# A long convolution beside a gated MLP on one core: the loads of the later chunks issued by GpSimd into its own queue

## The chip, the core and the metric

The kernel runs on one core of a Trainium2 chip. A core has five engines that work through instruction streams of their own, each in order: TensorE (PE in the profile, its weight loads PEld), VectorE (DVE), ScalarE (ACT), GpSimd (POOL) and SyncE (SP). They wait for each other through semaphores. Transfers between the main memory and the core's own memory run on 16 DMA engines. An instruction of SP, ACT or POOL starts them, and the profile shows those of SP as SPq. The metric is the time on the device in microseconds (us); less is better.

## The reference, cut to what matters

```python
xn = layernorm(A_q)                              # 2048 rows of 640, bf16
# part A: a long convolution with gates
k_shift = sum over t<4 of k[s-t] * shift_k[:, t] # a short filter along the rows
kv = k_shift * v
y  = irfft(rfft(kv padded) * rfft(ssm_k padded)) # each column with its filter of 2048 taps
y  = y + kv * ssm_D
A  = xn * y
# part B: a gated MLP, 640 -> 1728 -> 640
B  = (sigmoid(xn @ w_gate) * (xn @ w_up)) @ w_down
out = A_q + A + B
```

## The kernel before, in words

**Rows and blocks.** A row index is written p·16 + b, with p one of 128 partitions and b one of 16 blocks. x, xn, k, v and the result have this form in the core's memory. Four blocks make a group, and the MLP runs over the four groups t = 0 to 3.

**The MLP.** For each group TensorE needs xn transposed (`xnT`). Group 0 is transposed on TensorE; for groups 1 to 3 a DMA transpose of each block does it (`xn_turn`, L240, issued by SP). For each of 13 slices of the hidden width, `gate_mm` and `up_mm` (five matmuls each, `product`, L260) fill one bank each of a pool of four in the matmul memory (`psG`); ACT takes the sigmoid (`gate_ev`, L269), DVE multiplies (`up_ev`, L275) into `hT`. A shared last slice is `both_*`. `down_mm` (L304) multiplies hT by `wd`, seven matmuls a call, and `down_ev` (L309, DVE) adds the result to x in place.

**The layer norm.** Per group: statistics (`ln_norms`, DVE L198 and L202), variance (`ln_var`, L210), the power −1/2 on POOL (`ln_pow`, L214), and `ln_xn` (DVE, L219) for each block.

**The convolution.** The columns are five chunks of 128. For each chunk c:
- loads: the filter `hn` in four DMAs and the D row `dr` (`load_h`, L136 and L139), the four taps of the short filter for all partitions (`load_taps`, L143), k in two halves (`load_k`, L155) with three rows from the partition before in two DMAs (`load_halo`, L159 and L160), and v in two halves (`load_v`, L169). k has two buffers (`kxs`, used by turns), v with the filter has two (`kvh`), and `hn`, `dr` and the taps have one each;
- `taps` (ACT, for chunk 0 POOL), sixteen steps `kv_op` on DVE (L337 to L346; eight for each half of the blocks), two transposes of the filter on DVE (`h_turn`, L323), and `add_D` on POOL (L317), which adds D to the filter's first tap;
- a transform in two stages by matmuls: `st1_mm` (eight calls, TensorE L363 and L365; those for block 0 wait for `add_D`), evacuated by `st1_ev`, written to main memory (`wr1`, L377) and read back in another layout (`rd2`, L387), `st2_mm` (L396) and `st2_ev`;
- the product of the two spectra on DVE (`prod`, L409 and L411), `inv1_mm` (L425), `inv1_ev`, again a trip through main memory (`wr2`, L441 and L445; `rdb`, L455), `inv2_mm` (L464, with the table `TBt`), and two DVE steps (`inv2_q` L469, `inv2_x` L474) that multiply with xn and add to x.

**The order.** Nothing is scheduled automatically. Each kind of step has a letter and a list of its own (`chains`), and the string `ORDER` says, letter by letter, which list gives the next step. The letters' order is therefore the program order, and with it the order on each engine and on each queue. `g` stands for gate, up and down products, `s` and `u` for their evacuations, `m` for the first loads, `n` for x's groups 2 and 3 and the table `TBt`, `h`, `T`, `K`, `V` for the chunk loads from chunk 2 on (taps from chunk 1), `k` for `kv_op`, `P` and `D` for the two POOL steps, `e` for the transposes, `w`, `r`, `W`, `R` for the trips through main memory. `F`, `J` and `I` are evacuations of `st2`, `inv1` and `st1` done by DVE instead of ACT. A step waits only for the data and buffers that it uses, but on its engine it stands behind every earlier step.

In the kernel before, SP issues all these transfers: 137 steps of these lists. POOL's list is nine steps long: taps 0, add_D 0, pow 1, add_D 1, add_D 2, pow 2, add_D 3, add_D 4, pow 3. (`pow 1` is `ln_pow` of group 1, and so on.)

Of the kernel before, what the change touches and what calls it, by code (L numbers as in the profile page):

```python
# [19 lines left out]
P = 128  # L20
NB = S // P
# [36 lines left out]
def kernel(  # L58
# [14 lines left out]
    nc = tc.nc  # L73
    xr = A_q.flatten_outer_dims().rearrange("(p b) d -> p b d", b=NB)
    kr = A_k.flatten_outer_dims().rearrange("(p b) d -> p b d", b=NB)
    vr = A_v.flatten_outer_dims().rearrange("(p b) d -> p b d", b=NB)
# [3 lines left out]
    Drow = A_ssm_D.rearrange("(o d) -> o d", o=1)  # L80

    s1bits, tbbits, smbits = _tables()
    srow = A_shift_k.rearrange("d m -> (d m)").rearrange("(o n) -> o n", o=1)
    S1d = nc.inline_tensor(s1bits, name="tabS1")
    TBd = nc.inline_tensor(tbbits, name="tabTB")
# [4 lines left out]
    dr = ctx.enter_context(tc.tile_pool(name="dr", bufs=1, space=bass.MemoryType.DRAM))  # L90
# [8 lines left out]
    TBt = res.tile([P, 2, NB, P], U16, name="TBt")  # L99
# [12 lines left out]
    kxs = [res.tile([P, NB + 3, P], BF16, name="kx%d" % i) for i in range(2)]  # L112
# [8 lines left out]
    sync = nc.sync  # L121
# [3 lines left out]
    cin = [dict() for _ in range(NC)]  # L125

    def load_x(eng, g, n=4):
        for b in range(4 * g, 4 * g + 4, n):
            eng.dma_start(x[:, b:b + n, :], xr[:, b:b + n, :])

    def load_h(c):

        d = cin[c]
        d["hn"] = cv.tile([P, 4, 512], BF16, name="hn")
        d["dr"] = cv.tile([1, P], BF16, name="dr")
        sync.dma_start(d["dr"][:, :], Drow[:, c * P:(c + 1) * P])  # L136
        for q in range(4):
            src = A_ssm_k[c * P:(c + 1) * P, 512 * q:512 * q + 512].rearrange("(k r) t -> r k t", k=4)
            sync.dma_start(d["hn"][32 * q:32 * q + 32, :, :], src)  # L139

    def load_taps(c):
        cin[c]["sraw"] = cv.tile([P, 4 * P], BF16, name="sraw")
        sync.dma_start(cin[c]["sraw"][:], srow[:, 4 * c * P:4 * (c + 1) * P].to_broadcast((P, 4 * P)))  # L143

    def taps(c):
        sc = cv.tile([P, 4, P], BF16, name="sc")
# [5 lines left out]
        cin[c]["sc"] = sc  # L152

    def load_k(c, lo, hi):
        sync.dma_start(kxs[c % 2][:, lo + 3:hi + 3, :], kr[:, lo:hi, c * P:(c + 1) * P])  # L155

    def load_halo(c):
        cs = slice(c * P, (c + 1) * P)
        sync.dma_start(kxs[c % 2][16:P, 0:3, :], kr[15:P - 1, NB - 3:NB, cs])  # L159
        sync.dma_start(kxs[c % 2][1:16, 0:3, :], kr[0:15, NB - 3:NB, cs])  # L160

    def slot(c):

        if "kvh" not in cin[c]:
            cin[c]["kvh"] = cv.tile([P, 2, NB, P], BF16, name="kvh", bufs=2)
        return cin[c]["kvh"]

    def load_v(c, lo, hi):
        sync.dma_start(slot(c)[:, 0, lo:hi, :], vr[:, lo:hi, c * P:(c + 1) * P])  # L169

    def load_w(eng, lo, hi, u):
        if u == 0:
# [348 lines left out]
    def step(k, fn, *args):  # L521
        chains[k].append((fn, args))
# [16 lines left out]
    def hs(c):  # L539
        return [(load_h, c)]  # L540

    def ks(c):
        return [(load_halo, c), (load_k, c, 0, 8), (load_k, c, 8, NB)]

    def vs(c):
        return [(load_v, c, 0, 8), (load_v, c, 8, NB)]

    for k in ((load_w, sync, 512, 768, 0),
              (load_w, sync, 512, 768, 1),
              (load_taps, 0),  # L550
              (sync.dma_start, SMt[:], SMd.ap()),
              (load_w, sync, 768, 1024, 0),
              (load_w, sync, 768, 1024, 1),
              (load_w, sync, 1024, 1280, 0),
              (load_w, sync, 1024, 1280, 1),
              (load_wd, sync, 0, 7),
              *ks(0),
              (load_w, sync, 1280, FF, 0),
              (load_w, sync, 1280, FF, 1),
              *hs(0),  # L560
              *vs(0),
              (load_wd, sync, 7, NFC),
              (sync.dma_start, S1t[:], S1d.ap()),
              *hs(1),
              (load_x, sync, 1),
              *ks(1),
              *vs(1)):
        step("m", *k)
    for k in ((load_x, sync, 2), (load_x, sync, 3), (sync.dma_start, TBt[:], TBd.ap())):
        step("n", *k)  # L570
    step("Z", taps, 0)

    for c in range(NC):
# [28 lines left out]
        if c == 0:  # L602
            continue
        step("T", load_taps, c)
        step("t", taps, c)
        if c > 1:
# [21 lines left out]
    step("o", store, NB - 1, NB, 4 * P, DM)  # L628

    ORDER = """  # L630
    mgmmmmgmgmgsummZmgmgsmmgugmssgkmmukgskgugkusgsugkkgkHggmmuskuggkHmssukgmDgggukskgukkksaTmmgauAgmkaAH
    HlglAalAlglmwgautAkagugmggPmwlkgAhglkelauleggkakukkugekAAuuDkHgkuaaekgkwgsATKugkAwgsnkkgskgtuKaKAuka
    gskkgauwgkAlDAakVgglkKkrsakAuwAgakgVsAgalswAkaguKgkkAurbgkBswksHgTBgkbtuguBBpkgawkgslaAgsuKkalupKgrA
    AgkahPlnHsAwugaglVasgkgVpAsTAKukDpuckwglkkCgaCaHAugkAkgkeklubkgrkBBgguuwkgbggkpghtBBrbkegleBgBaauegw
    HAparguVkApauAkgwpADWaugakksAngkugpkwlAsucgsgJlpkCulbrgBKBsgaAuapgpAgrbsFggBussWkukrlpcHgguPCCgbslkV
    ggBuBgbpslBkuBRdpgspgWqqcusdgCgkrkkrCsbqFugqBgubskgBRdwBuagpAaqAdgllWwrsewRpugaqgIaggrpAaAaqupgIqupg
    ddcCgeuqgJebgupegFRuBgqbBpgqBgWpdcrguqqgJqCrubwuwdrgFpBgsbqpggpWpqBugBpscsuJggCurpgbggRFBbsWpdsudupq
    rgBqgqBcqRJsgrpCgsbBuWguBpdspqgbuBBgpqdpsgcgrugCRJqbpggsduBqsBgupgspgWqRqcuJdqgsgCdoqgusqWgudggqgugo
    uRgquRggddouqqgguqddgqqqqoquqggoogouoogouoooo
    """  # L640
    left = {k: iter(v) for k, v in chains.items()}
    for k in "".join(ORDER.split()):
# [33 lines left out]
```

## Time and profile before

| | us |
|---|---|
| median of 3 runs (238.31 to 239.72) | 238.9 |
| the profiled execution | 237.94 |
| its span, first to last instruction | 236.2 |
| PE busy | 229.1 (97%) |
| DVE busy | 204.1 (86%) |
| ACT busy | 121.7 (52%) |
| POOL busy | 11.5 (5%) |
| mean busy share of the DMA engines, SP's queue | 90.3% |

The granted TensorE clock is 1.0 throughout. A busy time counts what an engine executes; DMA issues are not counted. In a line of the timeline the numbers are the start, the duration, the engine, the line of the program, the operation with what it writes and reads, a count, and in square brackets the idle time before it with what ended it. In the waits a line gives who waited for whom: the total, the number of times, the longest.

### The profile page before, as it was taken

Reading aid. Unit: us, or ns where it says so; the run is one execution under the profiler, and the core shown is the slowest. Engines: PE = TensorE matmul, PEld = TensorE weight load, DVE = VectorE, ACT = ScalarE, POOL = GpSimd, SP = SyncE. Lnnn points to the kernel's source line nnn. Section 1 sums busy time; section 2 is a strip of 40 time slices with the busy share of each in tenths; the row PEclk is TensorE's granted clock in tenths of the full one; section 3 lists DMA queues with packets and bytes.
Section 4 is the critical chain, followed back from the end, with each engine's and each line's share of the span. In section 5 each row is a group of like instructions: output and inputs, shape, how many; then the busy total and the mean of one; then the engine's idle time right before and its main releaser. Section 6 shows DMA issues by size and latency. Waiting matters only on the chain.

```text
span 236.2 us, 5433 instructions
## 1 busy us (share of the span) xinstructions
PE 229.1 (97%) x2205; PEld 131.2 (56%) x2205; DVE 204.1 (86%) x364; ACT 121.7 (52%) x152; POOL 11.5 (5%) x24
## 2 busy tenths in 40 slices
PE   7799999999899899999999999999999999999995
PEld 3664445877355445666754444478664344446772
DVE  3632898999969999999999999899999999988473
ACT  2343323633564897776776777653346367653000
POOL 5210000020100001000100010000000000000000
PEclk9999999999999999999999999999999999999999
DMA  6999999958899999899899996899989879556664
GB/s 211 292 313 237 259 308 299 257 174 163 223 317 269 321 253 270 225 286 217 228 232 321 248 265 186 240 246 271 235 260 284 238 186 255 160 155 177 191 212 134
DMA packets 97183, 56.79 MB, mean 240 GB/s; under 512 B 55878, under 2 KB 91270, under 8 KB 96902
## 3 DMA queue, kind: packets, MB, share of 16 engines
q1 hardware_dynamic: 96214, 55.62, 90.3%
q10 hardware_dynamic: 944, 0.82, 1.1%
q8 instruction: 17, 0.28, 0.5%
q14 instruction: 8, 0.07, 0.1%
HBM read 36.12 MB, written 18.35 MB: 231 GB/s over the span
## 4 chain that ended last, share of the span: by engine, by line
PE 84%; DVE 8%; DMA 4%; issue 1%; ACT 0%; ACTq 0%; DVEq 0%
PE pg L260 23%; PE pu L260 23%; PE pd L304 20%; PE psb L464 4%; PE ps L396 3%; DMA w<-in_B_w_up_dram 3%; PE ps L363 3%; PE ps L365 3%; PE psa L425 2%; PE pg L281 1%; DVE st L198 1%; DVE tmp L341 1%; DMA xnT<-xn 1%; DVE acc L343 1%; PE pu L251 1%
## 5 line engine op out<-in xcount | busy, mean ns | idle before, releaser
L260 PEld LDWEIGHTS <-w 128*128 128x128 bf16 x500 | 46.5, 98 | 55.8 <-issue 6.8
L304 PE MATMUL pd<-wd,hT 128*128 128x320 bf16 (+2 forms) x448 | 65.3, 299 | 0.0
L260 PE MATMUL pg<-xnT,w 128*128 128x512 bf16 x250 | 62.2, 380 | 0.9 <-DMA xnT<-xn 0.9
L260 PE MATMUL pu<-xnT,w 128*128 128x512 bf16 x250 | 62.2, 380 | 0.8 <-DVE hT L275 0.8
L304 PEld LDWEIGHTS <-hT 128*128 128x128 bf16 x448 | 41.9, 98 | 18.2 <-issue 2.3
L223 ACT CAST t<-ps 128x1024 bf16<-128x1024 f32 x38 | 37.8, 1016 | 23.6 <-PE ps L365 16.0
L269 ACT ACTIVATE sig<-pg 128x512 bf16<-128x512 f32 x52 | 31.1, 603 | 30.7 <-PE pg L260 27.7
L223 ACT CAST xz<-ps 128x1024 bf16<-128x1024 f32 x35 | 34.2, 1015 | 20.3 <-PE ps L396 20.3
L275 DVE TENSOR_TENSOR hT<-sig,pu 128x512 bf16<-128x512 bf16 x52 | 34.8, 675 | 9.6 <-PE pu L260 5.6
L411 DVE TENSOR_TENSOR xz<-xz 128x2048 bf16<-128x2048 bf16 x20 | 24.3, 1215 | 0.1
L365 PE MATMUL ps<-kvh,S1t 128*128 128x128 bf16 x160 | 21.7, 220 | 0.0
L363 PE MATMUL ps<-kvh,S1t 128*128 128x128 bf16 x160 | 21.6, 218 | 0.0
L341 DVE TENSOR_TENSOR tmp<-kx,sc 128x1024 bf16<-128x1024 bf16 x30 | 20.5, 683 | 0.4
L343 DVE TENSOR_TENSOR acc<-acc,tmp 128x1024 bf16<-128x1024 bf16 x30 | 20.5, 684 | 0.4
L309 DVE TENSOR_TENSOR x<-pd,x 128x320 bf16<-128x320 f32 (+2 forms) x32 | 15.2, 483 | 5.9 <-PE pd L304 5.7
L363 PEld LDWEIGHTS <-S1t 128*128 128x128 bf16 x160 | 15.5, 97 | 2.8 <-DVE kvh L346 0.3
L365 PEld LDWEIGHTS <-S1t 128*128 128x128 bf16 x160 | 15.4, 96 | 2.6
L198 DVE BATCH_NORM_STATS2 st<-x 128x6 f32<-128x320 bf16 x32 | 13.9, 476 | 2.7 <-DMA x<-in_A_q_dram 2.7
L469 DVE TENSOR_TENSOR yx<-psb,xn 128x512 bf16<-128x512 f32 x20 | 13.7, 684 | 1.4 <-PE psb L464 1.0
L409 DVE STREAM_SHUFFLE xz<-xz 128x512 f32<-128x512 f32 x20 | 14.5, 725 | 0.0
L223 ACT CAST ao<-psa 128x1024 bf16<-128x1024 f32 x11 | 10.8, 1014 | 5.8 <-PE psa L425 5.6
L464 PEld LDWEIGHTS <-TBt 128*128 128x128 bf16 x160 | 9.8, 98 | 3.0 <-issue 1.5
(48 smaller groups left out, 149.3 us busy)
## 6 DMA issues: line engine op xcount, KB each, us to landing
d<-t SPq DMA_DIRECT2D x20, 512.0 KB, 5.3
t<-d SPq DMA_DIRECT2D x20, 512.0 KB, 5.7
bi<-d SPq DMA_DIRECT2D x8, 512.0 KB, 4.8
d<-ao SPq DMA_DIRECT2D x6, 512.0 KB, 5.6
kx<-in_A_k_dram SPq DMA_DIRECT2D x10, 256.0 KB, 5.3
hn<-in_A_ssm_k_dram SPq DMA_DIRECT2D x20, 128.0 KB, 5.2
kvh<-in_A_v_dram SPq DMA_DIRECT2D x10, 256.0 KB, 5.4
x<-in_A_q_dram SPq DMA_DIRECT2D x3, 640.0 KB, 6.4
```

The costliest lines, as they stand in the source:

```text
L198: nc.vector.bn_stats(d["st"][:, i, s2, :], x[:, b, s2 * 320:(s2 + 1) * 320])
L223: nc.scalar.copy(out=out, in_=in_)
L260: nc.tensor.matmul(pg[:, :], lhsT=w[:, c, u * UP + fc * P:u * UP + (fc + 1) * P], rhs=xnT[:, :, c, :], start=(c == 0), stop=(c == NC - 1))
L269: nc.scalar.activation(sig[fc][:, :], pgs[0, fc][:, :], ACT.Sigmoid)
L275: nc.vector.tensor_tensor(hT[:, fc, :], sig[fc][:, :], pgs[1, fc][:, :], ALU.mult)
L304: nc.tensor.matmul(pd[:, :], lhsT=hT[:, fc, bb * P:(bb + 1) * P], rhs=wd[:, fc, es], start=(fc == 0), stop=(fc == NFC - 1))
L341: nc.vector.tensor_tensor(d["tmp"][:, :, :], kx[:, lo + 3 - m:hi + 3 - m, :], sb(m), ALU.mult)
L343: nc.vector.tensor_tensor(d["acc"][:, :, :], d["acc"][:, :, :], d["tmp"][:, :, :], ALU.add)
L363: nc.tensor.matmul(ps[:, i, 0:P], lhsT=S1[:, b, h, :], rhs=cin[c]["kvh"][:, 0, b, :], start=True, stop=True)
L365: nc.tensor.matmul(ps[:, i, P:2 * P], lhsT=S1[:, b, h, :], rhs=hp[:, b // 2, b % 2, :], start=True, stop=True)
L411: nc.vector.tensor_tensor(z[:, 1:3, :, :], z[:, 0:1, :, :].to_broadcast((P, 2, 8, P)), z[:, 1:3, :, :], ALU.mult)
L464: nc.tensor.matmul(ps[:, i, :], lhsT=TB[:, h, 4 * m + i, :], rhs=bi[:, h, 4 * (m % 2) + i, :], start=(h == 0), stop=(h == 1))
```

## The change

A helper `queue(c)` gives GpSimd's queue for chunks 2 to 4 and SP's for chunks 0 and 1, and every chunk load is issued through it. x's groups 2 and 3 and the table `TBt` are issued by GpSimd as well. That makes 39 DMA issues: for each of three chunks five of `load_h`, one of `load_taps`, two of `load_halo`, two each of `load_k` and `load_v`; two for x; one for the table.

```diff
+    def queue(c):
+        return nc.gpsimd if c > 1 else sync
+
     def load_h(c):
 ...
-        sync.dma_start(d["dr"][:, :], Drow[:, c * P:(c + 1) * P])
+        queue(c).dma_start(d["dr"][:, :], Drow[:, c * P:(c + 1) * P])
         for q in range(4):
 ...
-            sync.dma_start(d["hn"][32 * q:32 * q + 32, :, :], src)
+            queue(c).dma_start(d["hn"][32 * q:32 * q + 32, :, :], src)
 
     def load_taps(c):
 ...
-        sync.dma_start(cin[c]["sraw"][:], srow[:, 4 * c * P:4 * (c + 1) * P].to_broadcast((P, 4 * P)))
+        queue(c).dma_start(cin[c]["sraw"][:], srow[:, 4 * c * P:4 * (c + 1) * P].to_broadcast((P, 4 * P)))
 ...
     def load_k(c, lo, hi):
-        sync.dma_start(kxs[c % 2][:, lo + 3:hi + 3, :], kr[:, lo:hi, c * P:(c + 1) * P])
+        queue(c).dma_start(kxs[c % 2][:, lo + 3:hi + 3, :], kr[:, lo:hi, c * P:(c + 1) * P])
 
     def load_halo(c):
         cs = slice(c * P, (c + 1) * P)
-        sync.dma_start(kxs[c % 2][16:P, 0:3, :], kr[15:P - 1, NB - 3:NB, cs])
-        sync.dma_start(kxs[c % 2][1:16, 0:3, :], kr[0:15, NB - 3:NB, cs])
+        queue(c).dma_start(kxs[c % 2][16:P, 0:3, :], kr[15:P - 1, NB - 3:NB, cs])
+        queue(c).dma_start(kxs[c % 2][1:16, 0:3, :], kr[0:15, NB - 3:NB, cs])
 ...
     def load_v(c, lo, hi):
-        sync.dma_start(slot(c)[:, 0, lo:hi, :], vr[:, lo:hi, c * P:(c + 1) * P])
+        queue(c).dma_start(slot(c)[:, 0, lo:hi, :], vr[:, lo:hi, c * P:(c + 1) * P])
 ...
-    for k in ((load_x, sync, 2), (load_x, sync, 3), (sync.dma_start, TBt[:], TBd.ap())):
+    for k in ((load_x, nc.gpsimd, 2), (load_x, nc.gpsimd, 3), (nc.gpsimd.dma_start, TBt[:], TBd.ap())):
         step("n", *k)
```

The string `ORDER` is another one, too, with the same 845 steps. What follows from it on each engine:

- POOL's list has 33 steps: taps 0, halo 2, add_D 0, first half of k 2, add_D 1, pow 1, h 2, taps 2, x 2, first half of v 2, second half of k 2, second half of v 2, taps 3, halo 3, add_D 2, k 3 (first half), x 3, h 3, TBt, k 3 (second half), pow 2, v 3 (first half), halo 4, v 3 (second half), add_D 3, taps 4, k 4 (first half), h 4, v 4 (first half), add_D 4, k 4 (second half), pow 3, v 4 (second half).
- SP keeps the first loads, the chunks 0 and 1, the transposes, the trips through main memory and the stores, 113 steps. The transposes of group 1 stand behind the first half of v 1; the second half follows after them. `add_D 1` now precedes `pow 1` on POOL.
- PE has the same steps in another order in places: the first `st1_mm` of chunk 0 comes after three down calls of group 0 instead of one, the first `inv1_mm` after four down calls of group 1 instead of two, `st1_mm` of chunk 3 after six down calls of that group instead of four; some calls of stage 2 and of the second inverse stage are one to five places earlier or later.
- DVE and ACT follow these moves. DVE takes 15 evacuations instead of 14 (one of stage 1 fewer, one of stage 2 and one of the first inverse stage more), ACT one fewer. The second transpose of chunk 2's filter stands before the statistics of x's blocks 9 to 11 instead of behind two of them.

More of the change, by code (lines that the diff above doesn't have):

```diff
@@ L630 @@
     ORDER = """
[L631 to L639, printed above, removed]
+    mmmmmmmmmggggsmmsumggsguuZsgggmukksmgmskmukgkggkmuksHgsggumkuggskgukHgskgmkmuggmkTsksgKuugkDagaAgkmA
+    uaHKtHmwmagllllAglgDPkAuaAwmklllahuelgekAugekakkugaggAgkggkAakaukuewgkukmkkgsTggAkuwsngkVutAgaskwkgs
+    AKgaukgrHkaAgAualakswkgAagVguskrAgAbgkwTksuBkBskkguKDgskkHlkaagguAlAKkngbtwushungpkplBsBgaAwgaugkpKl
+    gksaupgAAPlglswkVslrgkuKaueaglHAwaggkkAAVDcwCggTkaCkukuaAgregHkkAbggkugBBKkuurpbBgeklgBkgpbpgBluBpeg
+    atawAkuWggskuaklpghuAwasgAAgaarluAkHrkggAcVskgkJupgsCbgDswBugkBuspaAaKklgPgpAbugBkFsWrgRkcVCCsgugpdH
+    rsbpBkgBugWqudbsgplkpgrBBcurgqRCsqJgbgWkwgukgswpBrBlubksBFqgusludapdqaglgeAaguggRqAeaquAwAappgAaepqe
+    ggIcgCuwguJbBgpFdgrbpqugWBuqdpqBrgcugJpqgrCbugpsRwBFggpbupgBdsrqBuWpgdqrcJspggqgCbuFRqBggsubpdsWugBB
+    gdprscCqgpJrqgbsuBgqFRgupsgbspudpgqrWBgBduqqRcpgJCqWgsqbsBugBgpugsRdpgpucsgqJqCWdgqgusqgudgqouggudRq
+    gqugoRogggqudguodqgqqdudoggqqqqgogqoouuoooooo
     """
```

## The prediction

> **What bounds the kernel now.** I read the page's busy times and slices first, then the windows by stage, the waits, and the timelines of SyncE's queue (SP), VectorE (DVE) and GpSimd (POOL).
>
> ```profile
> PE 229.1 (97%) x2205; PEld 131.2 (56%) x2205; DVE 204.1 (86%) x364; ACT 121.7 (52%) x152; POOL 11.5 (5%) x24
> ...
> DVE  3632898999969999999999999899999999988473
> ...
> DMA  6999999958899999899899996899989879556664
> ```
>
> ```profile
> core 0: us, PE busy (x) PEld busy (x) DVE busy (x) ACT busy (x) POOL busy (x), PEclk, DMA share, GB/s
> ...
> 37.00:60.00 23.00, 22.12 (x203) 16.48 (x202) 22.56 (x46) 9.74 (x11) 1.41 (x2) 1.00 0.89 208
> 60.00:80.00 20.00, 19.18 (x135) 10.58 (x135) 17.46 (x33) 12.19 (x17) 0.72 (x1) 1.00 0.99 285
> 80.00:100.00 20.00, 20.00 (x191) 10.54 (x189) 19.74 (x35) 15.70 (x20) 1.43 (x2) 1.00 0.94 255
> ...
> 200.00:220.00 20.00, 20.00 (x220) 10.71 (x205) 16.92 (x27) 9.34 (x12) 0.00 (x0) 1.00 0.56 157
> ```
>
> TensorE (PE) is full; DVE is nearly full from 30 to 200 us; the DMA engines are busy about nine tenths. POOL is idle. PE's own work is not touched by the change, so a gain can only come out of PE's waits, and they are few:
>
> ```profile
> DVE acc L337 <- DMA kx<-in_A_k_dram: 4.7, 2, 2.9
> ...
> PE pg L260 <- DMA xnT<-xn: 0.9, 1, 0.9
> ...
> PE pu L260 <- DVE hT L275: 0.8, 1, 0.8
> ```
>
> After 20 us these two PE waits are the only ones over 0.3 us. The first, at 59.1 us, opens block 1: its last transpose is late. SP's timeline says why:
>
> ```profile
> 50.55 0.26 SPq L136 DMA_DIRECT2D dr<-in_A_ssm_D_dram  x1
> 50.90 2.35 SPq L139 DMA_DIRECT2D hn<-in_A_ssm_k_dram  x4
> 53.36 5.27 SPq L240 DMA_TRANSPOSE xnT<-xn  x4
> ...
> 62.16 2.63 SPq L155 DMA_DIRECT2D kx<-in_A_k_dram  x2
> ```
>
> The first normalised block was ready at 50.84 (DVE L219), but chunk 2's filter load stood ahead of the transposes; its D row waited for POOL's add of chunk 1, which itself ran behind `pow`. The second PE wait, at 76.8 us, is DVE being late, and DVE had lost time here:
>
> ```profile
> 69.21 0.69 DVE L337 TENSOR_TENSOR acc<-kx,sc 128x1024 bf16<-128x1024 bf16 x1 [1.73 <-DMA kx<-in_A_k_dram]
> ```
>
> Chunk 2's k was issued at 62.16 and DVE stood 1.73 us for it.
>
> **The change, part by part.** The sum is against the profiled execution, 237.94 us with a span of 236.2; the median of the runs is 238.9, 0.96 above it, and I add that at the end.
>
> *Off SP.* 39 DMA issues leave SP (per chunk 5 of h, 1 of taps, 2 of halo, 2 of k, 2 of v, three times; x twice; TBt). SP's rows for them add up to some 30 us between 50.5 and 134. Block 1's transposes then follow from xn's first tile: 51.0 + 5.27 for four + 1.4 from the last issue's end (58.63) to PE's start (60.05) = 57.7, and PE had finished its earlier work at 59.1. The wait of 0.9 goes whole; what is late next is PE itself. Of the other moves past SP (wr1's writes and rd2's reads run sooner by an issue or two) PE has no wait to recover: 0.
>
> *Chunk 2's k early.* On POOL it needs only k buffer 0, free after DVE's last read of it at 40.6. That halos wait for the rows they overwrite alone is seen in SP's row of 82.57 (chunk 4's halo), before the last DVE read of the same buffer at 83.03. So k of chunk 2 lands long before 67.5, DVE gets 1.73 us back, and PE's 0.8 goes: −0.8.
>
> *What an issue costs POOL.* No row shows one. Ends: SP's fastest issue of the same k load, 0.39 us, and SP's slowest, 2.93. For a value I take POOL's only element-by-element row: `pow` takes 0.563 us on one column and 1.016 on four, so 0.412 + 0.151 a column of 128. A load of 1,024 runs of 256 B (half of a k or v chunk) is 8 columns for the source and 8 for the target: 0.41 + 16 x 0.151 = 2.83. One of 128 runs (a quarter of h, taps, x, TBt): 0.71. Both halo loads: 1.7. One h group with its D row: 3.3. The value sits at the upper end, since the software row is nearer in kind. All 39: 3 x (4 x 2.83 + 3.3 + 0.7 + 1.7) + 2.1 = 53 us, inside 110 us in which POOL computes 5: POOL has room, and only its order can hurt. Queued behind a POOL load are `add_D` (TensorE's stage 1 waits for it), `pow` (the xn tiles on DVE wait for it) and the next loads. Place by place, with the times of before:
>
> - add_D 0 behind chunk 2's halo: released near 29.6, done by 32; stage 1 of chunk 0 starts after 40. Nothing.
> - pow 1 behind k of chunk 2 and add_D 1: 40.6 + 2.83, add_D 1 at 44.2; pow's input comes at 49.0. Nothing.
> - pow 2 behind h 3 (which needs DVE's second transpose of chunk 2's filter), TBt and k: 3.3 + 0.7 + 2.8 = 6.8. In the new order DVE has between that transpose and the first xn of group 2, start to start in its timeline, 3 statistics of 1.0, 5 convolution steps and 5 hT products of 0.60, and two shuffles and products of 0.62 + 1.14: 12.6 us. With pow's own 1.0 that leaves 4.8.
> - add_D 3 behind va3, halo 4, vb3: from pow 2's end at 91.95, 2.83 + 1.7 + 2.83 + 0.42 = 99.7. Stage 1 of chunk 3, now two down products later, starts near 102.4. 2.7 to spare; this place decides from 2.83 + 1.35 = 4.2 us a k or v load.
> - second half of k, chunk 4, behind add_D 4: 0.42 + 2.83 + the landing. SP's k loads landed 3.7 to 4.9 us (shortest, median) after issue, with 0.5 of it the issue: 6.5 to 7.7. Between the filter transpose that frees add_D 4 and the step that needs this half DVE has 4 x 0.60 + 3 x 0.60 + 1.14 + 0.62 + a cast of 1.14 = 7.1. A wait of 0 to 0.6, taken as 0.3.
>
> *xn beside POOL's issues.* POOL now writes while DVE normalises. That the two engines exclude each other is in POOL's rows:
>
> ```profile
> 49.11 1.02 POOL L214 TENSOR_TENSOR rstd<-var,mhalf 128x4 f32<-128x4 f32 x1 [17.25 <-DVE var L210]
> 50.10 0.42 POOL L317 TENSOR_TENSOR kvh<-kvh,dr 1x128 bf16<-1x128 bf16 x1
> 60.10 0.72 POOL L317 TENSOR_TENSOR kvh<-kvh,dr 1x128 bf16<-1x128 bf16 x1 [9.58 <-DMA xnT<-xn]
> ...
> 114.36 1.16 POOL L317 TENSOR_TENSOR kvh<-kvh,dr 1x128 bf16<-1x128 bf16 x1 [19.22 <-DMA xnT<-xn]
> ```
>
> The add of 0.42 took 0.72 and 1.16 where DVE ran a two-input operation, and ended 0.28 us after that one's end both times (60.54 and 115.24). The other way round, DVE's operations beside pow at 49.11 kept their length (0.68 and 0.49). So the price on DVE lies between 0 and every xn of groups 1 and 2 waiting for a load being written: 3 x 0.71 behind h 2, then 1.6 left of va3 and 2.83 of vb3, 6.5 together. I take one such meeting, 0.7: pow 1 releases the first xn and POOL's next load at the same moment. The Trainium skill, "SBUF — State Buffer", section "Who interferes with whom", goes further: a VectorE operation in a two-port mode, which tensor_scalar can enter, and a GpSimd operation lock each other out for the whole instruction. By that rule the term is nearer 6.5 than 0.7; the rows beside pow don't bear it out for DVE's side.
>
> *Two queues, one set of DMA engines.* The bytes are the same. Loads start earlier and share with the round trips (d<-t 5.3 us to landing, t<-d 5.7). PE waits for none of them now, so there is nothing to gain; taken as 0, the other end being the 3 us of the rival below.
>
> *The steps moved.* PE's list is the same set in another order. One evacuation goes from ACT to DVE: +1.22 there, inside the 3 us that DVE has free between 120 and 200. If that cover is gone, +1.2.
>
> Sum: −0.9 − 0.8 + 0.3 + 0.7 = −0.7, so 237.2 for a profiled execution and 238.2 beside the median.
>
> **Rivals.**
>
> *POOL falls behind (slower).* If a k or v load costs POOL over 4.2 us, add_D 3 holds PE. At 5 us and 0.71: +1.6 there (two loads of 0.8 more), +2.2 at k of chunk 4, less what overlaps, some +3; at 6 us and 1.2 a plain load, pow 2's group takes 6.0 + 1.2 + 6 = 13.2 and the 12.6 us are used up, va3 and k of chunk 3 are late too: +10 and over. Times 241 to 250. For it: software writes the runs, and no row bounds it. Against: POOL's columns cost 0.15.
>
> *xn held out (slower).* The 6.5 of above in stretches where DVE is busy 22.56 of 23 and 19.74 of 20, so most of it passes on: 238.2 − 0.7 + 2 to 6.5, about 241.5.
>
> *Transfers collide (slower).* Early loads take a turn each on engines that are 0.9 busy. If each round trip lands 1 us later, the last groups of a chunk come late where stage 2 has least room, 2 to 3 us in all: 240.5 to 241. The Trainium skill, "DMA: Bandwidth & Descriptors", section "Issuing engines are not separate DMA queues", speaks this way: issuing from several engines saves only issue time. That the trace agrees is seen in the one place where issue time did cost something, the transposes.
>
> *It does not do what it says.* DVE or PE take the freed time in other small waits, as both are full anyway: 238.9.
>
> *Whole gain.* Both waits go, no meeting costs anything: 238.9 − 1.7 = 237.2. Below 236.9 there is nothing to take.
>
> **How the numbers follow.** Within 0.5% is 1.2 us either way, about what a measurement of this kernel can tell from no change. The forecast, with its small prices anywhere between nothing (the whole gain) and twice the value, has 0.48 and a range of its own of 237.0 to 239.3; half of it lies below 237.7: 0.24 faster, 0.24 same. No effect 0.12, same. POOL behind 0.21, of it 0.01 too little to be told (same); xn held out 0.11 and collision 0.08. Slower 0.20 + 0.11 + 0.08 = 0.39, same 0.24 + 0.12 + 0.01 = 0.37. The likeliest single case is the forecast, 238.2. The range goes from the floor, 236.9, to 243.5, which leaves out the larger prices of the first rival.
>
> **What the changed profile would show.** Right: no PE wait for xnT near 59; no DVE wait for kx near 67 to 69; POOL issue rows of 0.4 to 2.9 us; add_D 3 done before stage 1 of chunk 3. Wrong: a PE wait of L363 on POOL L317, a DVE wait of L219 on POOL L214, L219 longer than 0.45 us, L337 waiting for kx after 120, or landings of t<-d well over 5.7.

## The result, and the profile after

The changed kernel took 252.75 us (median of 6 runs, 251.01 to 255.5) against 238.97 us for the kernel before (6 runs): a ratio of 1.0552, 95% interval 1.0513 to 1.0591. The ratios here and below leave out single slow runs (here the one of 255.5 us), while the times are medians of all runs. The forecast was 238.2 us with a range to 243.5: the time is 14.6 us above it and outside the range. Lines of the changed program carry numbers 3 higher than before from `load_h` on (L263 is the product that was L260).

The page of the changed kernel, busy times, slices and DMA queues (packets, MB, time of the packets as a share of 16 engines' span):

```profile
span 250.1 us, 5454 instructions
...
PE 231.9 (93%) x2205; PEld 132.4 (53%) x2205; DVE 206.2 (82%) x365; ACT 120.4 (48%) x151; POOL 39.9 (16%) x63
...
PE   8799999994089999999979999999999999999994
...
PEclk9999999999569999999999999999999999999999
...
q1 hardware_dynamic: 79900, 47.86, 73.6%
q0 software_dynamic: 2448, 7.77, 12.7%
```

PE has two slices of standstill after 58 us, and a lower granted clock behind them. The windows name the stage (the rows answer those shown of before):

```profile
core 0: us, PE busy (x) PEld busy (x) DVE busy (x) ACT busy (x) POOL busy (x), PEclk, DMA share, GB/s
37.00:60.00 23.00, 22.11 (x204) 16.44 (x201) 22.53 (x45) 9.53 (x11) 9.43 (x13) 1.00 0.93 227
60.00:80.00 20.00, 10.56 (x46) 4.65 (x47) 8.27 (x14) 4.57 (x7) 1.87 (x3) 0.74 0.77 162
80.00:100.00 20.00, 19.90 (x161) 10.36 (x160) 18.67 (x35) 15.33 (x21) 6.39 (x10) 1.00 0.81 247
```

From 60 to 80 us PE worked 10.56 us where it had worked 19.18. The waits of PE, and its timeline where it starts again:

```profile
PE pg L263 <- DMA xnT<-xn: 11.3, 2, 10.3
...
PE ps L399 <- DMA t<-d: 1.1, 1, 1.1
```

```profile
69.44 2.29 PE L263 MATMUL pg<-xnT,w 128*128 128x512 bf16 x5 [10.33 <-DMA xnT<-xn]
71.53 2.16 PE L263 MATMUL pu<-xnT,w 128*128 128x512 bf16 x5
```

Block 1's products, at 60.05 us before, start at 69.44, after a wait of 10.33 us for the transposes, and their first two groups of five take 2.29 and 2.16 us where 1.24 is usual. The two queues' timelines around it, SP's and POOL's:

```profile
51.16 6.79 SPq L243 DMA_TRANSPOSE xnT<-xn  x4
```

```profile
50.58 0.61 POOL L139 DMA_DIRECT2D dr<-in_A_ssm_D_dram  x1
51.20 2.36 POOL L142 DMA_DIRECT2D hn<-in_A_ssm_k_dram  x4
53.55 0.56 POOL L146 DMA_DIRECT2D sraw<-in_A_shift_k_dram  x1
54.10 0.57 POOL L129 DMA_DIRECT2D x<-in_A_q_dram  x1
54.64 0.93 POOL L172 DMA_DIRECT2D kvh<-in_A_v_dram  x1
55.54 0.91 POOL L158 DMA_DIRECT2D kx<-in_A_k_dram  x1
56.42 0.91 POOL L172 DMA_DIRECT2D kvh<-in_A_v_dram  x1
```

SP issued the transposes at 51.16, 2.2 us sooner than before, as the prediction wanted. But in the same 7 us POOL issued ten loads, 2.0 MB. The transposes of the whole kernel landed 4.3, 8.2 and 13.8 us after issue (shortest, median, longest) where it had been 2.6, 4.4 and 6.2. What the 16 DMA engines did from 58 to 64 us, after the last transpose of block 1 was issued:

```profile
q0 software_dynamic: 283, 1.10, 87.5%
q1 hardware_dynamic: 456, 0.11, 10.3%
```

POOL's queue (q0) had 87.5% of the engines' time, SP's (q1), in which the awaited transposes stood, 10.3%.

The 13.9 us of span come apart by PE alone: its busy time is 2.8 longer (most of it at the low clock) and its waits add up to 15.0 us instead of 4.2, 10.8 more; together 13.6.

### The profile page after: what moved, and what is told of

Read it like the earlier page. It is cut to its first block, busy times and chain, and to the rows that moved or that the text cites. A ratio compares the mean times of both kernels' runs of the same rounds, so it can differ in the third digit from the quotient of the medians.

```text
span 250.1 us, 5454 instructions
## 1 busy us (share of the span) xinstructions
PE 231.9 (93%) x2205; PEld 132.4 (53%) x2205; DVE 206.2 (82%) x365; ACT 120.4 (48%) x151; POOL 39.9 (16%) x63
## 4 chain that ended last, share of the span: by engine, by line
PE 64%; DMA 15%; DVE 15%; issue 2%; ACT 1%; ACTq 0%; DVEq 0%
PE pu L263 19%; PE pg L263 19%; PE pd L307 12%; DMA xnT<-xn 10%; PE psb L467 4%; DMA w<-in_B_w_up_dram 3%; PE ps L399 2%; DMA d<-t 2%; PE psa L428 2%; DVE acc L346 2%; DVE kvh L326 2%; DVE tmp L344 2%; DVE hT L278 2%; DVE st L201 2%; PE ps L368 1%
## 5 line engine op out<-in xcount | busy, mean ns | idle before, releaser
L263 PEld LDWEIGHTS <-w 128*128 128x128 bf16 x500 | 46.9, 99 | 68.3 <-DMA xnT<-xn 11.6
L263 PE MATMUL pg<-xnT,w 128*128 128x512 bf16 x250 | 63.2, 384 | 11.3 <-DMA xnT<-xn 11.3
L307 PE MATMUL pd<-wd,hT 128*128 128x320 bf16 (+2 forms) x448 | 66.0, 299 | 0.0
L263 PE MATMUL pu<-xnT,w 128*128 128x512 bf16 x250 | 63.2, 384 | 0.0
L226 ACT CAST t<-ps 128x1024 bf16<-128x1024 f32 x39 | 38.4, 1013 | 16.9 <-PE ps L368 13.7
L226 ACT CAST xz<-ps 128x1024 bf16<-128x1024 f32 x34 | 33.2, 1014 | 16.5 <-PE ps L399 15.2
L368 PE MATMUL ps<-kvh,S1t 128*128 128x128 bf16 x160 | 21.2, 219 | 0.0
L366 PE MATMUL ps<-kvh,S1t 128*128 128x128 bf16 x160 | 21.2, 217 | 0.0
L201 DVE BATCH_NORM_STATS2 st<-x 128x6 f32<-128x320 bf16 x32 | 13.8, 473 | 2.6 <-DMA x<-in_A_q_dram 2.6
L472 DVE TENSOR_TENSOR yx<-psb,xn 128x512 bf16<-128x512 f32 x20 | 13.8, 688 | 2.1 <-PE psb L467 1.7
L226 ACT CAST ao<-psa 128x1024 bf16<-128x1024 f32 x10 | 9.9, 1013 | 9.2 <-PE psa L428 9.2
L467 PEld LDWEIGHTS <-TBt 128*128 128x128 bf16 x160 | 10.3, 98 | 3.1 <-issue 0.5
```

Source lines behind the costliest of these rows:

```text
L201: nc.vector.bn_stats(d["st"][:, i, s2, :], x[:, b, s2 * 320:(s2 + 1) * 320])
L226: nc.scalar.copy(out=out, in_=in_)
L263: nc.tensor.matmul(pg[:, :], lhsT=w[:, c, u * UP + fc * P:u * UP + (fc + 1) * P], rhs=xnT[:, :, c, :], start=(c == 0), stop=(c == NC - 1))
L307: nc.tensor.matmul(pd[:, :], lhsT=hT[:, fc, bb * P:(bb + 1) * P], rhs=wd[:, fc, es], start=(fc == 0), stop=(fc == NFC - 1))
L366: nc.tensor.matmul(ps[:, i, 0:P], lhsT=S1[:, b, h, :], rhs=cin[c]["kvh"][:, 0, b, :], start=True, stop=True)
L368: nc.tensor.matmul(ps[:, i, P:2 * P], lhsT=S1[:, b, h, :], rhs=hp[:, b // 2, b % 2, :], start=True, stop=True)
```

## The experiments

Two theories stood at first. A: the loads in GpSimd's queue hold up SP's transposes. B: the new order of the steps costs the time.

**The order alone, on SP.**

```diff
     def queue(c):
-        return nc.gpsimd if c > 1 else sync
+        return sync
```

(and x's groups and the table on SP as well)

> The changed order of steps, with every load back on SP's queue. Theory A (GpSimd's queue starves SP's transposes: the loads issued by it at 50.6 to 57.3 us hold the DMA engines while the transposes of block 1 want them): PE's wait of 10.3 us for xnT is gone or under 1.5 us, and so is the low clock behind it; 238 to 242 us. Theory B (the new order of the steps costs the time, whichever queue carries the loads): the wait stays, 248 us or more. In between (243 to 247 us), the two share it.

Measured: 237.14 us, ratio to before 0.9932 (0.9902 to 0.9962). SP's queue and PE's start in this kernel:

```profile
49.40 1.79 SPq L142 DMA_DIRECT2D hn<-in_A_ssm_k_dram  x4
51.30 5.59 SPq L243 DMA_TRANSPOSE xnT<-xn  x4
```

```profile
58.87 1.24 PE L263 MATMUL pg<-xnT,w 128*128 128x512 bf16 x5
```

The transposes are issued when they were in the changed kernel, and PE doesn't wait for them. B is out: the new order is a gain of 0.7% (the interval of its ratio stays below 1), and the queue costs 15.6 us beside it by the medians (252.75 less 237.14, from two sets of runs), 14.8 by the two ratios (1.0552 less 0.9932, of 238.7). This kernel is faster than both.

**The old order, with GpSimd's queue.** The string `ORDER` of before, with `add_D 1` put ahead of h 2.

> The order of steps of the kernel before, with only add_D 1 put ahead of h 2, and the loads of chunks 2 to 4, of x's groups 2 and 3 and of the inverse table issued by GpSimd. Theory A (GpSimd's queue starves the transposes): as GpSimd runs ahead of SP whatever the order, its burst again stands behind pow 1, PE waits for xnT 5 to 12 us, 245 to 253 us. Theory B (the new order): 237 to 241 us.

Measured: 247.67 us, ratio 1.0362 (1.0286 to 1.0437). PE waited 3.68 us for xnT, less than expected, and ran the next five products in 2.29 us; GpSimd's burst begins at 50.93 here too. A holds again, at a smaller size in this place; the time, 9.0 us above the 238.7 of before in the same set of runs, is inside what was expected. In the profiled execution the span is 7.2 us longer than before: PE's busy time is 3.8 longer and its waits 3.3.

**The burst held back.** POOL reads a word of each transpose ahead of h 2.

```diff
+    hold = res.tile([1, 4], BF16, name="hold")
+
+    def hold_loads():
+        nc.gpsimd.tensor_copy(hold[:, :], xnT[0:1, :, 0, 0])
```

(a step of its own in `ORDER`, after the fourth transpose, with h 2 behind it)

> The changed kernel, with one small copy on GpSimd (1x4 elements, added work) that reads a word of each of block 1's four transposes, put ahead of h 2's loads, so that GpSimd issues none of the burst until they have landed. Theory A: the transposes land in 6 to 7 us, at about 57 to 58 us, PE's wait of 10.3 us goes to under 1.5 us; 238 to 242 us, unless the burst then meets the writes and reads of the first stage (wr1, rd2) and gives some of it back there (up to 245). Theory B (the order): no change, 249 us or more. A theory C, that GpSimd's own work on descriptors and not the transfers hold up the transposes, expects the same as A here.

Measured: 243.5 us, ratio 1.0202 (1.0146 to 1.0258). The wait for xnT is gone; PE starts block 1 at 58.79. So without the burst the transposes, issued at 51.00, land in time. Of the 15.6 us that the queue costs, 6.4 are left. The waits from 55 to 80 us show where:

```profile
POOL hold L545 <- DMA xnT<-xn: 8.2, 1, 8.2
...
ACT sc L154 <- DMA sraw<-in_A_shift_k_dram: 5.2, 1, 5.2
...
PE ps L366 <- ACT t L226: 3.4, 2, 1.9
ACT t L226 <- DMA d<-t: 3.4, 2, 2.1
```

The burst, at 59 us now, meets the next transfers in line: the first stage's writes (d<-t) land late, ACT can't reuse its buffer t, and PE stands 3.4 us for ACT. The collision was moved, not removed. In the profiled execution, whose span is 4.9 us longer than that of the order on SP, PE's waits are 3.7 longer (7.3 against 3.6, with 1.6 of it for a read of stage 2) and its busy time 1.1. That the loads are the cause of these later waits as well is read from the profile; it wasn't tried by itself. Nor does this kernel tell the transfers from GpSimd's own work on issuing them (theory C); the runs below with ScalarE's and SP's queue show that such harm does not need GpSimd.

**The wait filled with work.**

```diff
-    def product(u, fc):
+    def product(u, fc, fill=0):
         pg = psG.tile([P, 512], F32, name=("pg", "pu")[u], tag="g")
+        for _ in range(fill):
+            nc.tensor.matmul(pg[:, :], lhsT=w[:, 0, 0:P], rhs=w[:, 0, 0:512], start=True, stop=True)
 ...
-        pgs[0, fc] = product(0, fc)
+        pgs[0, fc] = product(0, fc, 40 if (t, fc) == (1, 0) else 0)
```

> The changed kernel, with 40 matmuls of 128x512 added on PE (into the tile that block 1's first gate product then overwrites, 8.6 us at 0.215 us each) into the wait for xnT. The wait ahead of the first product shrinks to 1 to 3 us, but block 1's products start no sooner. If the first ten products' 2.2 us longer run (2.29 and 2.16 us for five where 1.24 is usual) comes of PE having stood still, they run at 1.1 to 1.3 us for five and the time is 1.5 to 2.5 us under the changed kernel's 252.75 (250.2 to 251.3). If it comes of something else, no change (252 to 254).

Measured: 251.4 us, ratio 1.0557 (1.0486 to 1.0627), against 1.0552 without the filling: no difference that these runs can tell. The mechanism is there all the same:

```profile
59.10 8.58 PE L263 MATMUL pg<-w 128*128 128x512 bf16 x39
67.52 1.24 PE L265 MATMUL pg<-xnT,w 128*128 128x512 bf16 x5
```

```profile
123.17 0.66 PE L401 MATMUL ps<-t,SMt 32*32 32x512 bf16 x16 [3.21 <-DMA t<-d]
```

(39 of the 40 are in the trace.) The products start at full speed, 1.24 us for five. They also start 1.9 us sooner than in the changed kernel, which was not expected: in this execution the transposes landed 11.2 us after issue at the longest, against 13.8. So the time won by then, nearly 4 us, is only in part the clock's. Some 2 us of it were stood off again 56 us later, 3.21 us for a read of stage 2 that took 1.05 without the filling, with a low clock again (0.66 us for what takes 0.43). The low clock follows PE's standstill; what it costs in the end depends on the next transfer. The Trainium skill, "TensorE: Matmul & The Clock Gate", Part 1, says that the array drops to half its clock after an idle window of some 3.4 us and takes about as long of steady work to come back. The runs here agree in the main: waits of 3.7 us and more for xnT were followed by a granted clock of 0.50 and 2.29 us for five, a wait of 1.5 us (below) by 1.24; the full clock was back 2.7 to 5.9 us after PE's start.

**What it is in the second queue.** Is it the length of GpSimd's packets (3.2 KB in the mean, 0.6 KB on SP's queue), that GpSimd fills the queue, or the bytes? Four kernels add 1,664 KB of loads (1.70 MB as the profile counts, 1.64 in the expectations) to the order on SP, at the moment of the transposes, through two queues and in two shapes.

```diff
+    def extra():
+        nc.scalar.dma_start(TBt[:], TBd.ap())
+        nc.scalar.dma_start(x[:, 12:16, :], xr[:, 12:16, :])
```

> Added work on top of the changed order with all loads on SP's queue (237.14 us, no wait for xnT): 1.64 MB of loads in long rows (the inverse table, 8 KB to a row, and x's last group, 5 KB to a row; both are loaded again later as usual), issued by ScalarE into its own hardware queue just when SP issues the transposes of block 1 (about 51 us). Theory size (the engines take turns between queues packet by packet, and long packets take the turn for longer): transposes held up as by GpSimd's queue, PE waits 4 to 10 us for xnT, 241 to 250 us. Theory software (only a queue that GpSimd fills does that): wait under 2 us, 237 to 240 us. Theory bytes (any 1.64 MB costs its transfer time, about 4 us at the 415 GB/s that the trace reaches): wait 2 to 4 us, 239 to 242 us, and the same in all four kernels of this set.

The same with `nc.gpsimd`:

> The same 1.64 MB in long rows, issued by GpSimd behind pow 1 (about 50.5 us). Theories size and software: PE waits 4 to 10 us for xnT, 241 to 250 us. Theory bytes: 2 to 4 us, 239 to 242 us.

```diff
+    def extra():
+        for i in range(2):
+            nc.scalar.dma_start(TB[:, i, :, :], kr[:, :, i * P:(i + 1) * P])
+        nc.scalar.dma_start(x[:, 12:16, :].rearrange("p b d -> p (b d)").rearrange("p (n m) -> p n m", n=NB), kr[:, :, 256:416])
```

> 1.64 MB of loads in short runs (256 and 320 bytes, columns of k read into the same places as in the kernels with long rows, overwritten later), issued by ScalarE into its own hardware queue at about 51 us. Theory size: its packets are as short as those of the transposes, so these get half the turns: landing from 3 to about 5 us, PE waits 0 to 3 us, 237 to 240 us. Theory software: the same, 237 to 240 us. Theory bytes: as with long rows; since short packets move fewer bytes in their time, rather more, 3 to 6 us, 240 to 243 us.

The same with `nc.gpsimd`:

> The same short runs issued by GpSimd. In the trace of the changed kernel GpSimd's queue moved such loads in packets of 3.2 KB in the mean. Theory size: as its packets are long again, PE waits 4 to 10 us, 241 to 250 us; should the packets be short here, 0 to 3 us. Theory software: 4 to 10 us in either case. Theory bytes: 3 to 6 us.

Measured (the time of the extra load is its queue's share of 16 engines, times the span; ScalarE's own queue has 1.1% without it; the delay is the start of block 1's first product less 58.87):

| extra 1.70 MB | us, ratio to before | extra load on the engines | wait for xnT | delay of block 1 |
|---|---|---|---|---|
| ScalarE, long rows | 243.82, 1.020 (1.013 to 1.027) | 2.0% of 241.8 = 4.8 | 4.9 | 6.1 |
| GpSimd, long rows | 242.07, 1.013 (1.006 to 1.020) | 2.2% of 240.1 = 5.3 | 4.2 | 4.2 |
| ScalarE, short runs | 245.17, 1.029 (1.018 to 1.040) | 3.6% of 243.2 = 8.8 | 4.4 | 7.1 |
| GpSimd, short runs | 251.9, 1.052 (1.044 to 1.059) | 4.2% of 250.4 = 10.5 | 12.9 | 13.1 |

The last kernel's queue line and wait; it loses 14.8 of the changed kernel's 15.6 us by one load of three DMAs:

```profile
q0 software_dynamic: 464, 1.70, 4.2%
```

```profile
PE pg L263 <- DMA xnT<-xn: 12.9, 1, 12.9
```

All three theories miss. It is not software queues alone: ScalarE's hardware queue does it too. It is not the length of packets alone: 256-byte runs from ScalarE delayed block 1 by 7.1 us, where 0 to 3 of wait were expected. And it is not the bytes, which are equal. What sets the short runs apart from the long rows is the time that the extra load itself takes on the DMA engines: 4.8 and 5.3 us in long rows, with delays of 6.1 and 4.2, and 8.8 and 10.5 in short runs, with delays of 7.1 and 13.1. It is a rough measure: between the two kernels with long rows the order is the other way round.

In ScalarE's two kernels the transposes were held up already at issue. A wait of SP with the long rows:

```profile
SPq L243 <- DMA kvh<-in_A_v_dram: 6.0, 1, 6.0
```

SP issued them at 58.19 instead of 51.30, though DVE had finished their four blocks of xn by 52.7; the profile puts the wait down to a load of v that had been issued ahead of them and landed late. The transposes don't read v, and why SP waited for it is not shown. With the short runs on ScalarE's queue it is alike: by the profile SP waited 4.1 us for that load within h 2 and 3.6 us for the extra load ahead of the transposes, which left at 58.78. (The delays are longer than the waits for xnT there by 1.2 and 2.7 us; waits of PE in stage 1 came ahead, and with the short runs ScalarE itself was issuing until 58.86.)

In GpSimd's two kernels the transposes left on time, at 50.97 and 51.37, but SP's issue of the four took 9.84 and 11.61 us instead of 5.59. The row with the short runs:

```profile
51.37 11.61 SPq L243 DMA_TRANSPOSE xnT<-xn  x4
```

From the first issue to PE's start it was 12.1 and 20.6 us, against 7.6 in the order alone, and 6.8 and 7.2 in ScalarE's two kernels.

The Trainium skill, "DMA: Bandwidth & Descriptors", section "Queues, rings and completion order", has each DMA engine take turns between queues packet by packet. The rows of 58 to 64 us in the changed kernel (283 long packets with 87.5% of the time, 456 short ones with 10.3%) fit that. With the short runs on ScalarE's queue the packets were short on both sides, and from 58 to 62 us, when the first transposes were out, that queue still had nearly all of the engines:

```profile
q10 hardware_dynamic: 2750, 0.80, 92.9%
q1 hardware_dynamic: 119, 0.03, 4.1%
```

That is not packet for packet, 2,750 of ScalarE's (q10) to 119 of SP's (q1), unless SP's queue had little to offer at that time, which no run tells. How the engines share between two queues, and why GpSimd's short runs cost so much more than ScalarE's, is left open by these runs.

**The place in line.** A new theory: on one queue, transfers are served in the order of issue, and the engines are full; so a load delays the transposes by its own time if it gets ahead of them or beside them, and not if it stands behind them. The test puts the short runs on SP's own queue, once behind and once ahead of the four transposes (`nc.sync` in `extra`, the step after the fourth `xn_turn` or before the first).

> Added work on the changed order with all loads on SP (237.14 us): the 1.64 MB of short runs of the two kernels before, issued on SP's own queue right behind block 1's four transposes. New theory (place in line): transfers on SP's queue are served in the order of issue, so what stands behind the transposes can't delay them; a second queue's transfers go beside or ahead of them and delay them by about their own time on the DMA engines. PE waits under 1 us for xnT; the first stage's writes behind the load come 8 to 9 us later instead, which the casts' two buffers pass on: 239 to 247 us. Theory bytes (1.64 MB more at this time costs the transposes its time whatever its place): wait 4 to 9 us.

Measured: 244.12 us, ratio 1.0235 (1.02 to 1.0269). Block 1 starts at 59.20 with no wait for xnT. The loss comes 12 us later, from what now stands behind the extra load, chunk 1's v:

```profile
PE ps L366 <- DVE kvh L349: 5.2, 1, 5.2
```

```profile
DVE kvh L349 <- DMA kvh<-in_A_v_dram: 6.5, 1, 6.5
```

The victim was expected to be the writes d<-t; PE stood for the load of v. The writes were late as well: ACT stood 8.5 us for one.

> The same load on SP's queue right ahead of the four transposes. Place in line: the transposes wait for the whole load, 8.75 us by the time that these runs took of the 16 engines from ScalarE's queue (3.6% of 243.2 us); PE waits 7 to 10.5 us for xnT, 246 to 251 us. If it is the second queue as such that hurts, 0 to 3 us here.

Measured: 246.83 us, ratio 1.0356 (1.0302 to 1.0411), and block 1 starts 7.8 us late:

```profile
PE pg L263 <- DMA xnT<-xn: 7.4, 1, 7.4
```

SP's own rows show where the 7.8 us went:

```profile
51.53 4.10 SPq L544 DMA_DIRECT2D TBt<-in_A_k_dram  x2
55.68 2.27 SPq L545 DMA_DIRECT2D x<-in_A_k_dram  x1
58.05 7.09 SPq L243 DMA_TRANSPOSE xnT<-xn  x4
```

SP was issuing the load until 57.95, so that the transposes left 6.75 us later than in the order alone; from there to PE's start it was 8.6 us, against 7.6. No second queue is needed for the harm: the same load, queue and bytes cost the transposes 0.3 or 7.8 us, by their place. On one queue most of that was paid while SP issued; that the engines serve in the order of issue fits both runs, but isn't told apart from the time to issue.

**Parts of the change.** Chunk 2 and x's group 2 back on SP (`c > 2` in `queue`), the rest with GpSimd:

> The changed kernel with only chunk 2's loads and x's group 2 put back on SP, behind block 1's transposes; the loads of chunks 3 and 4, x's group 3 and the inverse table stay with GpSimd. Place in line: block 1's wait of 10.3 us and the low clock go; what GpSimd's loads do to the later transposes and to t<-d stays (2.0 us of waits in the changed kernel, maybe more now that everything is earlier): 237.5 to 242 us. If GpSimd's queue cost its time everywhere: 243 us or more.

Measured: 242.95 us, ratio 1.0191 (1.0132 to 1.0251), between the two expectations and next to the worse one. Block 1 starts at 58.83 without a wait. The remaining loads hurt elsewhere; at 117 us PE stands for a read of stage 2:

```profile
117.24 0.44 PE L399 MATMUL ps<-t,SMt 32*32 32x512 bf16 x16 [3.37 <-DMA t<-d]
```

Only x's two groups and the table with GpSimd:

> The changed kernel with only x's groups 2 and 3 and the inverse table left to GpSimd (2.3 MB in rows of 5 and 8 KB), all of the chunks' loads on SP. The 640 KB of x's group 2, issued at about 50.5 us, take 2.1 us of the 16 engines by the 5.3 us of 1.64 MB in long rows; so the transposes land 1.5 to 2.5 us later and PE waits 1 to 2.5 us for them, with a low clock behind it worth 0 to 2 us: 238 to 241.5 us. If it is rather the short-run loads of k and v alone that do harm, no wait and 236.5 to 238 us.

Measured: 243.87 us, ratio 1.0224 (1.019 to 1.0258): slower than expected. The wait for xnT is as foreseen, and at full clock behind it, but a second one follows at 81 us:

```profile
61.20 1.24 PE L263 MATMUL pg<-xnT,w 128*128 128x512 bf16 x5 [1.48 <-DMA xnT<-xn]
...
81.43 0.60 PE L399 MATMUL ps<-t,SMt 32*32 32x512 bf16 x2 [2.25 <-ACT t L226]
```

That one comes 10 us after GpSimd issued x's group 3 and the table (71.28 and 71.86 us), 1.7 MB, and ACT's 4.2 us of waiting for a write d<-t stands between them. Loads in long rows do harm as well.

## Why the prediction was wrong

**The step that failed is "Two queues, one set of DMA engines", "taken as 0, the other end being the 3 us".** Its sentence "Loads start earlier and share with the round trips" looked at d<-t and t<-d alone, whose median landings in fact hardly moved (5.3 to 5.6 and 5.7 to 5.2 us; the longest d<-t went from 6.4 to 12.6). The transposes, the transfers that PE waits for soonest, were left out. Its measured size is 15.6 us (252.75 less 237.14), against 0, with 3 as the far end. Of it 9.3 went (252.75 less 243.5) when the burst was held back until block 1's transposes had landed; the other 6.4 stayed, by the waits at later transfers. The mechanism had been named as the rival "Transfers collide"; that rival had the wrong victim, a fifth of the size and a chance of 0.08. The DMA share of 0.9 to 1.0 in the windows shown of before was a warning: on engines that full, an earlier load is somebody else's later one. A narrower window of the kernel before would have given the size:

```profile
50.00:58.00 8.00, 8.00 (x70) 6.01 (x69) 7.93 (x18) 2.02 (x2) 0.52 (x2) 1.00 0.63 128
```

While the transposes were issued the engines were 0.63 busy, so some 3 of these 8 us were free. The 2.0 MB that POOL put there take some 8.7 us at the 240 GB/s that the kernel before moves in the mean (an estimate). Full engines by themselves are not the harm: in the order on SP they are 0.99 busy in the same stretch, and the transposes land in time.

**"Off SP": the wait of 0.9 goes with the new order, and one of 10.3 comes with the queue.** Its 57.7 was built from the issue times with the 1.4 us to PE's start that before had shown, as if that landing time stayed. With everything on SP block 1 starts at 58.87 and the 0.9 goes, though no load has left SP; with GpSimd's queue PE starts at 69.44. The wait had come from the place of h 2 ahead of the transposes, which the new order mends by itself: on SP its four loads are out at 51.2 us instead of 53.25. The reason given, that 39 issues leave SP, was not needed.

**"Chunk 2's k early": right in what it wins.** DVE's waits for kx after the start-up are gone in the changed kernel and in the order on SP, and PE's 0.8 with them. But on SP too the first half of k is issued by 43.6 us, so the place in the order does it and not GpSimd. With the queue's harm taken away, the gain is 0.68% of 238.7, or 1.6 us, beside the 0.9 + 0.8 = 1.7 of these two steps. That they come so close is in part luck: the profiled execution of the order on SP has a new PE wait of 1.0 us (for ACT, ahead of the first inverse stage), its PE waits add up to 3.6 instead of 4.2, and its span is only 0.4 shorter.

**"What an issue costs POOL" was three times too high for k and v, and nearly twice in all.** A load of half a k or v chunk took 0.90 to 0.94 us against 2.83 (the lower row, SP's 0.39, was nearer); plain loads 0.53 to 0.61, against 0.71; POOL's busy time grew by 28.4 us, not 53. So none of the places where POOL might fall behind came near: no wait of PE or DVE for POOL is among the waits, but the 0.7 us at the start that before has too. The 0.3 for the second half of k 4 was nothing as well. So the first rival, with 0.21, came near in time by a mechanism that did not occur.

**"xn beside POOL's issues": next to nothing here, not 0.7.** The xn steps of the changed kernel have a median of 442 ns and a longest of 499, against 441 and 451 before. Such meetings do happen, though. In the old order with GpSimd's queue one xn step took 798 ns beside a load of k (POOL's 99.04 to 99.94), and beside GpSimd's extra load in short runs one took 1,015:

```profile
L222 DVE TENSOR_SCALAR xn<-x,mv,rstd x4: 429/506/1015, 50.6 to 52.6; 128x640 bf16<-128x640 bf16 x4
```

In the runs in which GpSimd issues no load the longest is 446 to 451. By the rule of the Trainium skill that was weighed there, "SBUF — State Buffer", section "Who interferes with whom", the later of the two would stand for the whole of the other's instruction. The traces show less: most xn steps beside POOL's issues kept 442 ns, and single ones lost 0.06 to 0.57 us, so the term taken, one meeting of 0.7, was of the right kind. POOL's `pow` took 1.36 to 1.94 us for 1.02, but 1.33 to 1.85 in the order on SP as well, so that is not the loads' doing.

**"The steps moved"** cost nothing that can be seen: DVE's busy time is 2.1 us longer, and the order on SP, which has the same steps, is still faster than before.

**What the prediction had no term for** is PE's clock: its busy time is 2.8 us longer, most of it in products behind its standstills.

## What to carry to other kernels

A queue is a place in line. Before a load is given a second queue, or an earlier place, look at the share of the DMA engines in that very stretch. Where the load's own time does not fit into what is free, list what else is in flight then and who waits for it, and charge the soonest-needed transfer with the load's own time on the engines, which here was 1.8 to 2.0 times as long for runs of 256 to 320 bytes as for rows of 5 to 8 KB. That charge is rough: loads of 4.8 to 10.5 us delayed the transposes by 4.2 to 13.1. And where a change moves both the order of steps and the queue, price the two apart: here the order was worth −0.7% and the queue +6.2% (1.0552 over 0.9932).

## What the runs showed of the hardware

- With the short runs on it, GpSimd's queue moved 1.70 MB in 464 packets in 10.5 us of all 16 engines (160 GB/s); with long rows in 288 packets in 5.3 us (320 GB/s). That its packets held 3.7 KB in the mean did not save the time of runs of 256 and 320 bytes.
- The issue of a load of 2,048 runs of 256 bytes on a hardware queue held its engine up to 4.99 us (ScalarE, the second of two; the first took 0.62), and 2.26 to 4.10 us for two on SP. GpSimd's issues of the same two took 2.56 us.
- A standstill of PE of 3.7 us or more for xnT was followed by 2.7 to 5.9 us at a granted clock of 0.50; 40 matmuls in the gap kept it up.
- Beside GpSimd's issues of loads in short runs, single `tensor_scalar` steps of 128x640 on VectorE took 798 and 1,015 ns where 442 is usual.
